# Decay attention with a squared-ReLU MLP on one core: the scores of the first fourteen heads as two rounded products

## The chip, the cores and the metric

The kernel runs on one core of a Trainium2 chip, as one launch. The core has five engines that run side by side and meet only at semaphores: TensorE (PE in the profile; PEld is its weight load), VectorE (DVE), ScalarE (ACT), GpSimd (POOL) and SyncE (SP), which here only issues DMAs. The metric is device time in microseconds for the whole launch, the median of three runs.

## The reference

For 8 batches of 8 heads (64 heads in all, 576 tokens, head size 64) it computes causal attention with a decay, and puts the joined heads through an MLP (4608 tokens, width 512, hidden width 2048):

```
scores = scale * q @ k^T + (cum_i - cum_j)      # cum = cumsum(log(clip(f, 1e-4, 1)))
scores = where(causal, -1e9, scores); scores -= max(scores, -1)
attn = exp(scores);  attn /= sum(attn) + 1e-9;  x = attn @ v
out = relu(x @ w_in) ** 2 @ w_out
```

Everything is float32 for the reader; the two MLP weights arrive as float64 and are turned into float32 inside the kernel.

## The kernel before

**Two kinds of product.** A matmul on float32 tiles goes through PE in several passes, as two MATMUL rows in the profile. A matmul on tiles marked F32R (rounded float32) is a single row, and its operands must have been written in that rounded type. Where a rounded product alone is too coarse, the kernel splits an operand into a rounded part and a rounded remainder and adds several rounded products in the same bank of PSUM. The MLP works like that (line 477: three products for x @ w_in, line 500: three for the second one), and so do all heads from head 14 on.

**Stages.** The work is laid out in slots, six for each head, one for each of six score units (`UNITS`: pieces of 320, 320, 192, 64, 448 and 256 columns, 1600 in all). In slot u of head h the program writes the score unit (line 337, `score`), its exp on ACT (line 362), and two slots later the product with v (line 392, `av_part`). During head h's slots the row maxima of head h+1 are made (`max_units`): six rounded matmuls (line 313), each followed on DVE by a masked maximum (line 319), and five of the results are sent by a small DMA each (line 325) from a column in SBUF into row 66 of the query operand of head h+1. The scores of head h+1 contract over that row too, so that they come out with the maximum already subtracted. Rows 64 and 65 carry the decay sums.

**The first heads.** For heads below `NWHOLE` = 14 the scores are one float32 matmul (line 346) on tiles called `rl`, which SP loads straight from memory (`load_whole`, line 259), plus a small mask matmul (line 348) where the unit crosses the diagonal. The maxima of these heads use a second copy of the same data, `rk`, which a GpSimd DMA rounds on its way (`load_rounded`, line 252). From head 14 on one load (`load`, line 237) brings the raw operands to `qkraw`; `prep` rounds them on DVE (lines 279 and 280) and ACT (281, 284) and makes the remainders on GpSimd (287, 290); the scores are two rounded products (lines 352 and 355).

**Weights.** There are 32 weight blocks of 512 KB. `weight_ops` issues the load of a block on SP (line 172) and converts it in five steps, on ACT (181, 209), DVE (192, 197, 202, 204) and GpSimd (210). `RATES` sets how many steps go into a slot: 1.2 in the slots of heads 0 to 7, 2.5 afterwards until all are done. MLP steps are mixed in from slot 60, the first slot of head 10, when the first batch has been divided by its row sums.

**What sets the order.** PE, ACT, DVE and GpSimd carry out their instructions in the order in which the program writes them (`in_order`). The order of SP is left to the scheduler. A queue works strictly in order: an instruction that waits holds everything behind it.

Of the kernel before, what the change touches and what calls it, by code (L numbers as in the profile page):

```python
# [17 lines left out]
def in_order(tc, engines):  # L18

    last = {}  # L20
    for i in tc.nc.cur_bb.bb.instructions:
# [12 lines left out]
def decay_attention_relu2_kernel(  # L34
# [37 lines left out]

    NWHOLE = 14
# [38 lines left out]
    def f32(x):  # L112
        return x if x.dtype == F32 else x.bitcast(F32)

    def constant_rows(engine, x, ones=True):

        engine.memset(f32(x[D:, 0]), -1.0 / SCALE)
        engine.memset(f32(x[D:, 1]), 0.0)
        if ones:
            k = f32(x[D:, 1])  # L120
            nc.gpsimd.affine_select(
                out=k, in_=k, pattern=[[0, S]], compare_op=ALU.not_equal, fill=1.0, base=-2,
# [11 lines left out]
    def decay():  # L134
        ft, zt, ct = (fr[:NH, i, :] for i in range(3))
        nc.vector.memset(zt, 0.0)
        constant_rows(nc.vector, rounded[0], False)
# [6 lines left out]
        chl = wk.tile([P, 2, S], F32R, name="qkraw", bufs=1)  # L144
        ch, cl = chl[:, 0, :], chl[:, 1, :]
# [8 lines left out]
    for x in vhs:  # L154
        nc.gpsimd.memset(x[:, :, D:D + 2].bitcast(F32), 1.0)
    constant_rows(nc.gpsimd, whole[0])
    constant_rows(nc.gpsimd, rounded[1], False)
    constant_rows(nc.gpsimd, whole[1])
# [5 lines left out]
    def weight_ops():  # L164
# [3 lines left out]
        def stage():  # L168
            i = len(staged)
            if i < NW:  # L170
                raw = staged[i] = wk.tile([P, 2 * DM], I32, name=f"w{i}", bufs=1)
                nc.sync.dma_start(out=raw, in_=(w_in, w_out)[i % 2][i // 2].bitcast(I32))
# [62 lines left out]
    def load(h):  # L235
        raw = wk.tile([P, 2, S], F32, name="qkraw", bufs=1)[:D]
        nc.sync.dma_start(out=raw, in_=qk[h])
        raws[h] = raw

    def load_cum(h, k):  # L240

        if h == 0:
            for i, c in enumerate(cum):
                nc.sync.dma_start(out=f32(k[D + i:D + i + 1, :]), in_=c[h:h + 1])
        else:
            nc.sync.dma_start(out=f32(k[D:D + 2, :]), in_=cum_dr[h])

    def load_rounded(h):

        x = rounded[h % 2]  # L250
        state[h] = dict(r2=x[:, 0], kl0=x[:, 1], p={})
        nc.gpsimd.dma_start(out=x[:D], in_=qk[h])
        if cum:
            load_cum(h, x[:, 1])

    def load_whole(h):

        x = state[h]["whole"] = whole[h % 2]
        nc.sync.dma_start(out=x[:D], in_=qk[h])
        if cum:  # L260
            load_cum(h, x[:, 1])
# [8 lines left out]
    def prep(h, part):  # L270

        if part == 0:
            x = wk.tile([P, 2, S], F32R, name="rl")
            (r2, kl0), (r1, l2) = ((x[:, 0], x[:, 1]) for x in (rounded[h % 2], x))
            st = state[h] = dict(r2=r2, kl0=kl0, r1=r1, l2=l2, p={}, raw=raws.pop(h))
            if h < NWHOLE + 2:
                nc.gpsimd.memset(f32(kl0[D:D + 32]), 1.0)
            load_cum(h, kl0)
            nc.vector.tensor_copy(out=r2[:D], in_=st["raw"][:, 0, :])
            nc.vector.tensor_copy(out=kl0[:D], in_=st["raw"][:, 1, :])  # L280
            nc.scalar.copy(out=st["l2"][D:], in_=st["raw"][:, 1, :])  # L281
        st = state[h]
        if part == 1:
# [430 lines left out]
```

## Time and profile before

| what | value |
|---|---|
| median of 3 runs | 1253.07 us (1252.28 to 1254.52) |
| profiled execution, its own time | 1255.36 us |
| its span, first to last instruction | 1253.3 us |
| busy: PE, DVE, ACT, GpSimd | 95%, 63%, 56%, 30% of the span |
| mean granted TensorE clock | 0.995 |

A row of the timeline reads: start, duration, engine, line, operation, output and input by the program's names, shapes, count (x2 where like rows were joined), and in brackets the idle time of the engine just ahead and what ended it. SPq rows are DMA issues on SP's queue. A row of the stretches reads: from:to, length, then for each engine its busy time and instruction count, the granted clock, the busy share of the DMA engines, and GB/s. A group row reads: line, engine, operation, tiles, shapes, count | busy us, mean ns of one | idle before it.

### The profile page before, as it was taken

To read this page: it belongs to the slowest core of one execution; us is meant where nothing else is said; L and a number is where in the kernel's file an instruction comes from. 1 tells how busy PE (TensorE), PEld (TensorE's weight loads), DVE (VectorE), ACT (ScalarE), POOL (GpSimd) and SP (SyncE) were. 2 spreads that over 40 slices of the span, in tenths; PEclk is the share of its full clock that TensorE was granted. 3 is DMA by queue.
4 is the path that set the end of the run, shared out by engine and by line. 5 is a ranking of instruction groups with operands and counts; after the bars stand their busy time and mean duration, and the time that the engine had idled before them with its cause. 6 is when DMAs were issued, how large, how long until landed. Compare 5 with 4: busy or idle time off the path is not lost.

```text
span 1253.3 us, 23182 instructions
## 1 busy us (share of the span) xinstructions
PE 1193.5 (95%) x7652; PEld 1051.8 (84%) x7652; DVE 785.1 (63%) x2042; ACT 702.0 (56%) x1720; POOL 372.4 (30%) x512
## 2 busy tenths in 40 slices
PE   3877899999999999999999999999999999999998
PEld 2544687888989899999899989998998989999997
DVE  7658776666666767666656566667665766532332
ACT  3545455556666666665565556666666666632332
POOL 4323223333333333333322233334333333200000
PEclk9999999999999999999999999999999999999999
DMA  8857631112121112121201121211121212000000
GB/s 199 193 129 176 177 87 26 51 32 57 41 55 33 48 37 57 40 57 26 55 18 52 31 57 32 55 34 52 40 57 41 57 41 52 17 27 1 18 18 17
DMA packets 115639, 71.90 MB, mean 57 GB/s; under 512 B 97384, under 2 KB 97384, under 8 KB 115520
## 3 DMA queue, kind: packets, MB, share of 16 engines
q1 hardware_dynamic: 114400, 66.30, 21.7%
q0 software_dynamic: 1120, 4.13, 1.5%
q8 instruction: 61, 1.00, 0.3%
q14 instruction: 58, 0.48, 0.1%
HBM read 60.20 MB, written 9.88 MB: 56 GB/s over the span
## 4 chain that ended last, share of the span: by engine, by line
PE 63%; ACT 1%; issue 1%; POOL 1%; DMA 0%; DVE 0%; SPq 0%; POOLq 0%; DVEq 0%; ACTq 0%
PE bank L477 25%; PE bank L500 24%; PE bank L388 3%; PE bank L355 2%; PE bank L390 2%; PE bank L389 2%; PE bank L313 2%; PE bank L352 2%; DMA den<-rdr 0%; ACT ph L377 0%; ACT den L426 0%; ACT r L485 0%; ACT p L362 0%; POOL v L299 0%; ACT rl L281 0%
## 5 line engine op out<-in xcount | busy, mean ns | idle before, releaser
L500 PE MATMUL bank<-w,gh 128*128 128x512 f32 x1152 | 413.8, 400 | 0.0
L477 PE MATMUL bank<-xh,w 128*128 128x256 f32 x2304 | 330.7, 286 | 4.9 <-DVE tcol L319 4.9
L378 DVE TENSOR_TENSOR pl<-p,ph 128x320 fp32r<-128x320 f32 (+4 forms) x300 | 186.9, 623 | 206.6 <-ACT ph L377 197.1
L477 PEld LDWEIGHTS bank<-xh,w 128*128 128x128 f32 x2304 | 301.2, 190 | 13.8 <-DVE tcol L319 5.3
L500 PEld LDWEIGHTS bank<-w,gh 128*128 128x128 f32 x1152 | 217.6, 189 | 39.0
L485 ACT ACTIVATE r<-bank 128x256 f32<-128x256 f32 x288 | 110.4, 383 | 211.7 <-PE bank L477 198.3
L500 PE MATMUL bank<-w,gl 128*128 128x512 f32 x576 | 227.1, 394 | 0.2 <-DVE gl L488 0.2
L486 DVE TENSOR_TENSOR g<-r 128x256 f32<-128x256 f32 x288 | 127.3, 442 | 144.2 <-ACT r L485 143.4
L364 POOL TENSOR_SCALAR_AFFINE_SELECT p<-p 128x128 f32<-128x128 f32 (+1 forms) x250 | 81.5, 326 | 454.2 <-ACT p L362 313.5
L377 ACT CAST ph<-p 128x320 fp32r<-128x320 f32 (+4 forms) x300 | 124.4, 415 | 148.9 <-POOL p L364 147.1
L477 PE MATMUL bank<-xl,w 128*128 128x256 f32 x1152 | 185.3, 283 | 0.0
L319 DVE CUSTOM_DVE_ANT_0 bank<-bank,mz 128x256 f32<-128x256 f32 (+4 forms) x320 | 133.7, 432 | 45.9 <-PE bank L313 44.5
L477 PEld LDWEIGHTS bank<-xl,w 128*128 128x128 f32 x1152 | 158.9, 191 | 0.0
L362 ACT ACTIVATE p<-bank 128x320 f32<-128x320 f32 (+4 forms) x300 | 115.8, 386 | 71.7 <-PE bank L355 67.3
L488 DVE TENSOR_TENSOR gl<-g,gh 128x256 fp32r<-128x256 f32 x288 | 128.9, 448 | 35.7 <-ACT p L362 0.9
L313 PE MATMUL bank<-rk 66*128 66x320 f32 (+9 forms) x384 | 111.8, 318 | 24.8 <-DMA rk<-qkraw 13.4
L487 ACT ACTIVATE gh<-r 128x256 fp32r<-128x256 f32 x288 | 120.5, 418 | 9.1
L500 PEld LDWEIGHTS bank<-w,gl 128*128 128x128 f32 x576 | 109.3, 190 | 14.3 <-DVE gl L488 0.9
L313 PEld LDWEIGHTS bank<-rk 66*128 66x128 f32 (+3 forms) x384 | 68.7, 185 | 40.1 <-DVE tcol L319 17.1
L388 PE MATMUL bank<-pl,vh 128*65 128x320 f32 (+4 forms) x350 | 99.4, 284 | 1.6 <-ACT den L426 1.4
L389 PE MATMUL bank<-ph,v 128*64 128x320 f32 (+4 forms) x350 | 94.8, 271 | 0.0
L390 PE MATMUL bank<-ph,vh 128*65 128x320 f32 (+4 forms) x350 | 93.0, 271 | 0.0
(71 smaller groups left out, 1498.2 us busy)
## 6 DMA issues: line engine op xcount, KB each, us to landing
qkraw<-in_qk SPq DMA_DIRECT2D x50, 288.0 KB
v<-in_v SPq DMA_DIRECT2D x64, 160.0 KB
den<-rdr SPq DMA_DIRECT2D x64, 144.0 KB
out<-osb SPq DMA_DIRECT2D x36, 256.0 KB
w<-in_w_in SPq DMA_DIRECT2D x16, 512.0 KB
w<-in_w_out SPq DMA_DIRECT2D x16, 512.0 KB
rl<-in_qk SPq DMA_DIRECT2D x14, 288.0 KB
rk<-in_qk POOLq DMA_DIRECT2D x14, 288.0 KB, 4.7
```

Source lines behind the costliest of these rows:

```text
L313: nc.tensor.matmul(ps[:m, :n], st["r2"][:rows, q0:q0 + m], st["kl0"][:rows, k0:k0 + n], start=True, stop=True,)
L319: nc.vector.tensor_tensor_reduce(out=ps[:m, :n], in0=ps[:m, :n], in1=mz[:m, mo:mo + n], op0=ALU.add, op1=ALU.min, scale=-1.0, scalar=init, ...
L377: nc.scalar.copy(out=ph[:kn, :n], in_=p[:kn, :n])
L378: nc.vector.tensor_tensor(out=pl[:kn, :n], in0=p[:kn, :n], in1=ph[:kn, :n].bitcast(F32), op=ALU.subtract,)
L388: nc.tensor.matmul(acc[:D + 1, o], vh, pl[:kn, i], start=first, stop=False)
L389: nc.tensor.matmul(acc[:D, o], vl, ph[:kn, i], start=False, stop=False)
L390: nc.tensor.matmul(acc[:D + 1, o], vh, ph[:kn, i], start=False, stop=last)
L477: nc.tensor.matmul(ph[:, :T], w[:, s, cc], x[:, cc, :], start=(cc == 0 and k == 0), stop=(cc == NCC - 1 and k == 2),)
L486: nc.vector.tensor_tensor(out=g, in0=r, in1=r, op=ALU.mult)
L487: nc.scalar.activation(out=gh, in_=r, func=AF.Square)
L488: nc.vector.tensor_tensor(out=gl, in0=g, in1=gh.bitcast(F32), op=ALU.subtract)
L500: nc.tensor.matmul(po, g[:, ts], w[:, s], start=(fc == 0 and k == 0), stop=(fc == NF - 1 and k == 2),)
```

## The change

- The scores of heads 0 to 13 become two rounded products, `kl0` with `r2` over all 128 rows and `l2` with `r1`, with the mask matmul between them where there was one. The product with v of these heads stays float32.
- For heads 0 to 7 (`NDEEP` = 8) the rounded copies `r2` and `kl0` come from GpSimd DMAs, now two for each head, into three sets of tiles instead of two; the raw operands come by `load` into `qkraw` (even heads) or the tile of `xt1` (odd heads). ACT makes two copies and DVE two remainders for each of these heads.
- Heads 8 to 13 are prepared like the later ones: rounded by DVE from the raw load, remainders on GpSimd, and their maxima are made in slots 1.5 to 4 instead of 0 to 2.5.
- `load_whole` and the `rl` tiles of the first heads are gone, and with them 14 loads of 288 KB.
- The 32 weight loads are issued from ACT's queue.
- At the start the constant rows are written in another order, and the DMAs of the decay sums on SP are kept in the order of writing.

```diff
-    rounded = [cpool.tile([P, 2, S], F32R, name=f"rk_{i}") for i in range(2)]
-    whole = [wk.tile([P, 2, S], F32, name="rl") for _ in range(2)]
+    r2s = [cpool.tile([P, S], F32R, name=f"r2_{i}") for i in range(2)] + [spare("xh0")]
+    kl0s = [cpool.tile([P, S], F32R, name=f"kl0_{i}") for i in range(2)] + [spare("xl0")]
...
-                nc.sync.dma_start(out=raw, in_=(w_in, w_out)[i % 2][i // 2].bitcast(I32))
+                nc.scalar.dma_start(out=raw, in_=(w_in, w_out)[i % 2][i // 2].bitcast(I32))
...
+            if h < NDEEP and h % 2:
+                raw = wk.tile([P, NCC, S], F32, name="xt1", bufs=1)[:D, :2]
+            else:
+                raw = wk.tile([P, 2, S], F32, name="qkraw", bufs=1)[:D]
+            nc.sync.dma_start(out=raw, in_=qk[h])
...
+        r2, kl0 = r2s[h % 3], kl0s[h % 3]
+        nc.gpsimd.dma_start(out=kl0[:D], in_=qk[h, :, 1, :])
+        nc.gpsimd.dma_start(out=r2[:D], in_=qk[h, :, 0, :])
...
+        eng = nc.vector if h < NDEEP else nc.gpsimd
         if part == 2:
-            nc.gpsimd.tensor_tensor(out=l2, in0=k, in1=st["kl0"][:D].bitcast(F32), op=ALU.subtract)
+            eng.tensor_tensor(out=l2, in0=k, in1=st["kl0"][:D].bitcast(F32), op=ALU.subtract)
         if part == 3:
-            nc.gpsimd.tensor_tensor(out=r1[D:], in0=q, in1=r1[:D].bitcast(F32), op=ALU.subtract)
+            eng.tensor_tensor(out=r1[D:], in0=q, in1=r1[:D].bitcast(F32), op=ALU.subtract)
...
-        if h < NWHOLE:
-            masked = q0 == k0
-            r, k = st["whole"][:, 0], st["whole"][:, 1]
-            nc.tensor.matmul(ps[:kn, :n], k[:, k0:k0 + kn], r[:, q0:q1], start=True, stop=not masked)
+        rows = P if h < NWHOLE else D + 3
+        nc.tensor.matmul(
+            ps[:kn, :n], st["kl0"][:rows, k0:k0 + kn], st["r2"][:rows, q0:q1], start=True, stop=False,
+        )
+        if h < NWHOLE and q0 == k0:
+            nc.tensor.matmul(
+                ps[:kn, :kn], mz[:kn, MW - P:MW - P + kn], eye[:kn, :kn], start=False, stop=False,
+            )
+        nc.tensor.matmul(
+            ps[:kn, :n], st["l2"][:, k0:k0 + kn], st["r1"][:, q0:q1], start=False, stop=True,
+        )
...
-    SPLIT = 0, 1, 1, 3
-    LOAD = 4
+    SPLIT = (0, 1, 2, 3), (0, 1, 1, 3)
+    LOAD = 3, 4
...
+        deep = h < NDEEP
+        for part in range(4):
+            at((h - 1) * NU + SPLIT[not deep][part], 1, prep, h, part)
+        if h > 1:
+            at((h - 2) * NU + LOAD[not deep], 0, load, h)
+        if deep and h > 1:
+            at((h - 2) * NU, 1, load_rounded, h)
+            at((h - 2) * NU, 1, load_cum, h)
-        for i, x in enumerate(MAXIMA[split]):
+        for i, x in enumerate(MAXIMA[not deep]):
```

How the instructions stand now is shown at three places. The first is SP's queue where it sends the maxima of a head (`tcol` is the column of maxima). Before, during head 2, the maxima of head 3 go into `rl`:

```order
L325 DMA rl<-tcol 1x128x1
L436 DMA cmp<-den 64x1x9 x2
L325 DMA rl<-tcol 1x128x1 x3
L172 DMA w_428<-in_w_in 128x1024
L266 DMA v<-in_v 128x5x64
L325 DMA rl<-tcol 1x64x1
```

Now, during head 2, the same maxima go into `r_0_76` (the query operand of head 3):

```order
L320 DMA r_0_76<-tcol 1x128x1
L256 DMA v<-in_v 128x5x64
L320 DMA r_0_76<-tcol 1x128x1 x2
L427 DMA cmp<-den 64x1x9
L320 DMA r_0_76<-tcol 1x128x1
L320 DMA r_0_76<-tcol 1x64x1
```

The load of v and the weight load no longer stand between the last maxima and their DMA.

The second place is DVE during head 1, from the first maximum of head 2 to the last. Before:

```order
L319 ISA bank_294,tcol<-bank_294,mz 128x256
L319 ISA bank_297,tcol<-bank_297,mz,tcol 128x320
L319 ISA bank_314,tcol<-bank_314,mz 128x448
L319 ISA bank_318,tcol<-bank_318,mz 128x320
L192 TENSOR_SCALAR wmag<-wmag 128x512
L319 ISA bank_330,tcol<-bank_330,mz 128x192
L197 TENSOR_SCALAR osb<-wmag 128x512
L319 ISA bank_341,tcol<-bank_341,mz 64x64
```

Now, with `l_320` and `r_347` the remainder tiles of head 2:

```order
L315 ISA bank_317,tcol<-bank_317,mz 128x256
L315 ISA bank_322,tcol<-bank_322,mz,tcol 128x320
L315 ISA bank_343,tcol<-bank_343,mz 128x448
L315 ISA bank_349,tcol<-bank_349,mz 128x320
L186 TENSOR_SCALAR wmag<-wmag 128x512
L315 ISA bank_362,tcol<-bank_362,mz 128x192
L191 TENSOR_SCALAR osb<-wmag 128x512
L284 TENSOR_TENSOR l_320<-qkraw,xl_81 64x576
L315 ISA bank_374,tcol<-bank_374,mz 64x64
L196 SCALAR_TENSOR_TENSOR osb<-w_177,osb 128x512
L287 TENSOR_TENSOR r_347<-qkraw,r_347 64x576
```

One remainder has come in ahead of the last maximum, the other behind it.

The third place is ACT around the first slots of head 1, where the exps of its first two units (`ph`, `pl`) are made. Before:

```order
L362 ACTIVATE ph<-bank_284 128x320
L425 COPY xt_289<-bank_237 64x320
L426 COPY den<-bank_237 1x320
L209 CAST w_301<-osb 128x512
L362 ACTIVATE pl<-bank_304 128x320
```

Now:

```order
L166 DMA w_304<-in_w_in 128x1024
L353 ACTIVATE ph<-bank_306 128x320
L416 COPY xt_312<-bank_256 64x320
L417 COPY den<-bank_256 1x320
L276 CAST l_320<-qkraw 64x576
L203 CAST w_329<-osb 128x512
L353 ACTIVATE pl<-bank_332 128x320
```

The copy into `l_320` and the weight load `w_304` are new among ACT's exps; the weight casts stood there already. With the waits shown, the weight loads on ACT read like this:

```order
L166 DMA w_248<-in_w_out 128x1024 [waits DMAHW3_49]
L166 DMA w_304<-in_w_in 128x1024 [waits DMAHW1_49]
L166 DMA w_397<-in_w_out 128x1024 [waits DMAHW2_49]
```

Each waits for the end of an earlier DMA on one of eight completion semaphores that ACT's and SP's loads share.

More of the change, by code (lines that the diff above doesn't have):

```diff
@@ L270, in prep @@
     def prep(h, part):
+        if h >= NH:
+            return
         if part == 0:
[L273 to L281, printed above, removed]
+            b = h % 3 if h < NDEEP else h % 2
+            raw = raws.pop(h)
+            if h >= NDEEP:
+                r2, kl0 = r2s[b], kl0s[b]
+                state[h] = dict(r2=r2, kl0=kl0, p={})
+                load_cum(h)
+                nc.vector.tensor_copy(out=r2[:D], in_=raw[:, 0, :])
+                nc.vector.tensor_copy(out=kl0[:D], in_=raw[:, 1, :])
+            st = state[h]
+            st["raw"] = raw
+            st["l2"] = wk.tile([P, S], F32R, name="l2")
+            nc.scalar.copy(out=st["l2"][D:], in_=raw[:, 1, :])
         st = state[h]
+        eng = nc.vector if h < NDEEP else nc.gpsimd
         if part == 1:
+            st["r1"] = wk.tile([P, S], F32R, name="r1")
             nc.scalar.copy(out=st["r1"][:D], in_=st["raw"][:, 0, :])
@@ L323, in unit @@
             if last:
-                r = st["whole"][:, 0] if h < NWHOLE else st["r2"].bitcast(F32)
-                nc.sync.dma_start(out=r[D + 2:D + 3, q0:end], in_=acc)
+                nc.sync.dma_start(out=st["r2"][D + 2:D + 3, q0:end].bitcast(F32), in_=acc)
         us = []
@@ L635, in decay_attention_relu2_kernel @@
     load_f()
+    load(0)
     load_rounded(0)
+    constant_rows(nc.vector, 0)
+    load_rounded(1)
     convert(1)
[L638 removed]
     decay()
[L640 to L641 removed]
+    begin = len(tc.nc.cur_bb.bb.instructions)
+    load_cum(0)
     store_cum()
[L643 to L644 removed]
+    in_order(tc, [mybir.EngineType.SP], begin)
+    load(1)
+    constant_rows(nc.gpsimd, 1, 2)
+    load_cum(1)
+    for x in vhs:
+        nc.gpsimd.memset(x[:, :, D:D + 2].bitcast(F32), 1.0)
     for n in range(-2 * NU, last_slot + 1):
```

82 lines of the change are left out of this document (22 added, 60 removed).

## The prediction

> **What bounds the kernel now.** I read the page first, then cut the span into stretches at the first scores of a head, then followed single heads on the timeline.
>
> ```profile
> PE 1193.5 (95%) x7652; PEld 1051.8 (84%) x7652; DVE 785.1 (63%) x2042; ACT 702.0 (56%) x1720; POOL 372.4 (30%) x512
> PE   3877899999999999999999999999999999999998
> ...
> 0.00:23.00 23.00, 3.04 (x7) 1.58 (x7) 17.54 (x34) 8.25 (x12) 10.84 (x25) 1.00 0.82 212
> 23.00:104.33 81.33, 63.90 (x291) 44.34 (x291) 49.51 (x148) 41.78 (x99) 24.30 (x31) 0.98 0.74 166
> 104.33:127.81 23.48, 18.39 (x75) 11.62 (x75) 20.34 (x46) 13.47 (x30) 8.77 (x10) 0.93 0.66 164
> 127.81:216.06 88.25, 80.49 (x463) 66.43 (x462) 64.87 (x143) 42.33 (x101) 26.93 (x25) 0.98 0.37 97
> 216.06:1253.30 1037.24, 1027.65 (x6824) 927.78 (x6822) 632.89 (x1671) 596.22 (x1480) 301.54 (x423) 1.00 0.16 40
> ```
>
> The 95% for PE is a mean over unlike stages. The five stretches are: the start; heads 0 to 7 (81.33 / 8 = 10.17 us a head); heads 8 and 9, where weight conversion runs at double rate; heads 10 to 13, with MLP steps mixed in; and everything from head 14 on, where PE is busy for 1027.65 of 1037.24 us. In the last stretch nothing but PE work counts. In heads 0 to 7 PE is busy for 79%, so something else ends a wait there. The change touches only the first 216 us.
>
> What a head waits for shows where head 1 ends, and in head 3:
>
> ```profile
> 37.34 0.22 DVE L319 CUSTOM_DVE_ANT_0 bank<-bank,mz 64x64 f32<-64x64 f32 x1
> 37.69 0.60 SPq L266 DMA_DIRECT2D v<-in_v  x1
> 38.38 0.59 SPq L325 DMA_DIRECT2D rl<-tcol  x1
> 39.74 0.51 PE L346 MATMUL bank<-rl 128*128 128x320 f32 x1
> ...
> 45.35 0.22 DVE L319 CUSTOM_DVE_ANT_0 bank<-bank,mz 64x64 f32<-64x64 f32 x1
> 47.62 0.60 SPq L172 DMA_DIRECT2D w<-in_w_in  x1
> 48.32 0.68 SPq L266 DMA_DIRECT2D v<-in_v  x1
> 49.09 0.59 SPq L325 DMA_DIRECT2D rl<-tcol  x1
> 50.13 0.78 PE L346 MATMUL bank<-rl 128*128 128x320 f32 x2 [2.19 <-DMA rl<-tcol]
> 51.55 0.70 PE L346 MATMUL bank<-rl 128*128 128x320 f32 x2
> 51.60 0.43 DVE L319 CUSTOM_DVE_ANT_0 bank<-bank,mz 128x256 f32<-128x256 f32 x1 [2.85 <-PE bank L313]
> 52.09 0.22 PE L348 MATMUL bank<-p,mz 128*128 128x128 bf16 x1
> 55.93 0.21 DVE L319 CUSTOM_DVE_ANT_0 bank<-bank,mz 64x64 f32<-64x64 f32 x1
> 57.00 0.60 SPq L266 DMA_DIRECT2D v<-in_v  x1
> 57.69 0.83 SPq L325 DMA_DIRECT2D rl<-tcol  x1
> 60.17 0.54 PE L346 MATMUL bank<-rl 128*128 128x320 f32 x1 [2.37 <-DMA rl<-tcol]
> ```
>
> It is a loop. Head 3 begins with its first score at 50.13; 1.47 us later DVE starts the first maximum of head 4 (51.60), because that matmul stands behind the score on PE; the last maximum ends on DVE at about 56.2, 4.6 us later; its row goes out on SP only at 57.69, behind the load of v; and when it has landed head 4 begins, 60.17. 1.47 + 4.6 + 4.0 is the 10.04 us of the head. In head 2 the tail from last maximum to next head was 4.5 us (45.6 to 50.13), with a weight load and a v load ahead on SP; at the end of head 1, 37.6 to 39.74, it was 2.1 us.
>
> **The change, part by part.**
>
> *PE.* The rows below give the price of a score unit before and in its new form, as head 14 has it already.
>
> ```profile
> 45.85 0.92 PE L346 MATMUL bank<-rl 128*128 128x448 f32 x2
> 46.60 0.22 PE L348 MATMUL bank<-p,mz 128*128 128x128 bf16 x1
> ...
> 216.06 0.32 PE L352 MATMUL bank<-rk 67*128 67x320 f32 x1
> 216.21 0.31 PE L355 MATMUL bank<-rl 128*128 128x320 f32 x1
> 216.36 0.70 PE L411 MATMUL bank<-ph,v 128*128 128x320 f32 x2
> ...
> 229.95 0.37 PE L352 MATMUL bank<-rk 67*128 67x448 f32 x1
> 230.15 0.37 PE L355 MATMUL bank<-rl 128*128 128x448 f32 x1
> 230.36 0.25 PE L388 MATMUL bank<-pl,vh 128*65 128x192 f32 x1
> ```
>
> Durations of PE rows overlap, so I take start to next start. A float32 unit of 320 columns holds PE from 51.55 to 52.09, 0.54 us, one of 448 from 45.85 to 46.60, 0.75 us: 1.68 ns a column. The pair of rounded products takes 0.30 and 0.41 us, 0.93 ns a column. Over the 1600 columns of a head that is 0.75 ns x 1600 = 1.2 us less. Where PE binds, it is worth 1.2 us a head; elsewhere only the first unit (0.54 - 0.30 = 0.24 us), which stands ahead of the first maximum in the loop.
>
> *Added work.* The rows of the same operations in the later heads and at the start:
>
> ```profile
> L287 POOL TENSOR_TENSOR rl<-qkraw,rk 64x576 fp32r<-64x576 f32 x50 | 72.3, 1445 | 0.2
> L281 ACT CAST rl<-qkraw 64x576 fp32r<-64x576 f32 x50 | 33.5, 670 | 0.7
> L280 DVE CAST rk<-qkraw 64x576 fp32r<-64x576 f32 x50 | 33.5, 669 | 0.0
> L279 DVE CAST rk<-qkraw 64x576 fp32r<-64x576 f32 x50 | 26.0, 520 | 0.0
> L252 POOL DMA_DIRECT2D rk<-in_qk x14 | 8.3, 590 | 14.2 <-PE bank L313 14.2
> 9.14 0.75 DVE L147 TENSOR_TENSOR qkraw<-xt,qkraw 64x576 fp32r<-64x576 f32 x1
> ...
> 145.50 1.26 POOL L210 TENSOR_TENSOR w<-osb,w 128x512 fp32r<-128x512 f32 x1 [9.04 <-ACT w L209]
> 145.66 1.43 DVE L197 TENSOR_SCALAR osb<-wmag 128x512 int32<-128x512 int32 x1
> ```
>
> ACT gets two copies a head (2 x 0.67 = 1.34 us). It also gets the weight loads: 1.2 steps a slot, six slots, five steps a block, so 1.44 blocks a head. The trace has no DMA issue on ACT; bounds are 0 and the 0.6 us of the longer issues on SP and POOL above, so up to 0.86 us a head, and I take 0.6 us each. ACT then has 41.78 / 8 + 1.34 + 0.86 = 7.4 us of work a head. DVE gets two subtractions of 0.75 us for heads 0 to 7: 49.51 / 8 + 1.5 = 7.7 us a head. Both still fit into a head of 9 to 10 us, but with little room. For heads 8 to 13 DVE gets two casts (0.52 + 0.67 = 1.19 us) and GpSimd two subtractions (2.9 us) each; the cost of the latter is also that DVE and GpSimd hold each other up, as in the last two rows, where an operation that elsewhere takes 0.43 us needed 1.43. GpSimd's DMAs for heads 0 to 7 are issued over five slots ahead of use, which covers their 0.59 us each and their landing.
>
> *Start.* PE begins with scores at 23.00. The change takes a weight load and a v load out from between the last rows of head 0 on SP, but puts a subtraction ahead of the last maximum, and makes one row of decay sums wait for the second weight load. I take 0; bounds -2 (three issues of 0.6) and +2 (the tail of 4.5 us instead of 2.1 us).
>
> *Heads 0 to 7.* The first part of the loop becomes 1.47 - 0.24 = 1.23 us; the second 4.6 + 0.75 = 5.35 us, because the first remainder stands ahead of the last maximum. The tail: on SP one `cmp` DMA and the row ahead (0.6 each, partly overlapped by DVE) remain, 0.9 us; from issue to the next head the three heads above took 1.4, 1.0 and 2.5 us; I take 2.0, since the DMA engines stay 74% busy. Tail 2.9 us, head 9.5 us. Against 10.17 that is 8 x -0.68 = **-5.4 us**. Bounds: with the tail of head 1 (2.1) a head is 8.7 us, -11.8; with that of head 3 (4.0) 10.6 us, +3.4.
>
> *Heads 8 and 9.* DVE is busy for 20.34 of 23.48 us and is the bound. Two heads of casts add 2.4 us; four GpSimd subtractions may each hold up a DVE operation by 1 us as above, say half of them, 2 us; some 2.4 of the 3.1 idle microseconds absorb part. **+2 us**, bounds -1 and +5.
>
> *Heads 10 to 13.* PE is busy for 80.49 of 88.25 us, so 4 x 1.2 = 4.8 us less PE work should nearly all arrive; DVE, at 64.87 us, gets 3 x 1.19 more and has room. **-4 us**, bounds -5 and +1 (a stall of DVE or GpSimd that the MLP waits for).
>
> *The rest.* The order of PE from head 14 on is unchanged, so is its length: 0, bounds -1 and +1.
>
> Sum: 0 - 5.4 + 2 - 4 = -7.4 us. Against the profiled execution that is a span of 1253.3 - 7.4 = 1245.9 and a time of 1255.36 - 7.4 = 1248.0. Its own time lies 2.3 us above the median of the runs, so for the median I predict 1253.07 - 7.4 = **1245.7 us**.
>
> One rule stands against the move of the weight loads. The Trainium skill, page "DMA: Bandwidth & Descriptors", section "Issuing engines are not separate DMA queues", says that DMAs started by different engines run on the same sixteen DMA engines and interleave, so that a second issuing engine saves only issue time. By that rule only the 0.6 us of the issue goes from the tail. The trace fits it half: at 0.74 mean busy share a row took 1.0 us to land in one head and 2.5 us in another.
>
> **The rivals.**
>
> *The tail stays (no change).* The row DMAs land as late as in head 3 because the DMA engines are as full as before, from whichever queue. For it: the 2.5 us from 57.69 to 60.17 are landing, not queueing on SP. Against it: 1.0 us in head 2 with a weight load and a v load just ahead. A head takes 10.6 us: +3.4 + 2 - 4 = +1.4, **1254.5 us**. It is also what the skill's rule gives.
>
> *ACT holds the loop (slower).* Place: the weight loads on ACT. They wait for an earlier DMA on a shared completion semaphore, and behind each stand the exps that the product with v and the score banks wait for. Price: with a landing of 1.7 us (mean of 1.0 and 2.5) for each, 1.44 x 1.7 = 2.4 us a head; if half of it delays the loop a head is 9.5 + 1.2 = 10.7 us, +4.2; with +3 and -3 in the next two stretches and +1 at the start, +5.2, **1258.3 us**. It decides from 0.7 us a head on, where 9.5 passes 10.17. For it: ACT has 7.4 us of work in the loop. Against: the DMA waited for was issued most of a head earlier.
>
> *The tail is always short (faster).* All heads like head 1: -11.8, heads 8 and 9 at +1, heads 10 to 13 at -4.8, start -1: -16.6, **1236.5 us**. For it: SP loses six issues in four heads. Against: head 1 was bound by PE, and it had only one DMA ahead on SP.
>
> That the change does not do what it says is excluded by the order: all 32 weight loads stand on ACT, and the float32 score matmuls are gone.
>
> **How the numbers follow.** Forecast 0.45 (its own range 1241 to 1250), no change 0.20, slower 0.20, faster 0.15. I call 0.2%, 2.5 us, what a measurement can tell, so faster is below 1250.6 and slower above 1255.6. Faster: 0.15 + 0.43 = 0.58; the same: 0.02 + 0.16 = 0.18, and 0.02 from the slower case; slower: 0.18 + 0.04 = 0.22. The range reaches to the fast and the slow case: 1237 to 1257 leaves 0.1 on each side.
>
> **What would show it.** Right: first scores of heads 0 to 7 about 9.5 us apart, the subtraction ahead of the last 64x64 maximum, a tail of about 3 us; the stretch from head 10 to head 14 about 4 us shorter; from head 14 on the same 1037 us. Wrong: PE waiting for ACT's exps, ACT idle ahead of a weight load, or heads above 10.2 us apart.

## The result and the profile after

The changed kernel takes 1272.15 us (median; 1269.88 to 1273.47) against 1253.8 us of the kernel before on the same chip. The ratio is 1.0135 (95% interval 1.0104 to 1.0165), so by the ratio it is slower by about 17 us, where 7 us less was forecast and the range ended at 1257. The profiled execution has a span of 1271.1 us, 17.8 more than before.

The busy times, the granted clock and the stretches of the changed kernel, cut at the first scores of heads 0, 8, 10 and 14 as in the prediction:

```profile
PE 1199.7 (94%) x7652; PEld 1060.2 (83%) x7652; DVE 808.9 (64%) x2070; ACT 717.9 (56%) x1748; POOL 388.1 (31%) x523
PEclk9887699999999999999999999999999999999999
...
0.00:25.79 25.79, 3.04 (x7) 1.58 (x7) 13.92 (x32) 8.01 (x12) 11.00 (x24) 1.00 0.83 205
25.79:109.79 84.00, 68.04 (x290) 49.73 (x290) 66.13 (x165) 50.31 (x114) 30.19 (x37) 0.85 0.61 147
109.79:142.94 33.15, 22.13 (x75) 15.31 (x75) 25.46 (x55) 17.41 (x37) 14.55 (x13) 0.65 0.47 133
142.94:237.30 94.36, 81.28 (x460) 67.81 (x461) 74.45 (x149) 46.00 (x106) 33.08 (x28) 0.93 0.26 73
237.30:1271.10 1033.80, 1025.26 (x6824) 925.75 (x6822) 628.96 (x1671) 596.22 (x1480) 299.29 (x423) 1.00 0.16 40
```

Against the stretches before, the start is 2.8 us longer, heads 0 to 7 are 2.7, heads 8 and 9 9.7, heads 10 to 13 6.1 longer, and the rest is 3.4 us shorter. PE is idle for 11.0 of 33.2 us in heads 8 and 9 (before 5.1 of 23.5) and for 13.1 of 94.4 in heads 10 to 13 (before 7.8 of 88.3). The granted clock falls to 0.65 in heads 8 and 9.

**What one profile can tell.** The runs below include kernels that are alike up to head 7, but for a load or a remainder in that head's slots, and so show how far one profile scatters. Heads 0 to 7 took 84.0, 81.0, 79.7 and 80.4 us in four kernels with the change's code there, mean 81.3, and 81.3, 82.6, 83.1, 77.4 and 82.9 in five with the code before, mean 81.5. The start took 24.0 to 25.8 in the first four, mean 24.9, and 22.7 to 25.0 in the others, mean 23.4. The rest took 1033.7 to 1035.9 us in nearly all other kernels; in the profile of before it took 1037.2, with head 17 20.1 us long instead of 18.4. What stands out of this scatter is heads 8 to 13, some 16 us; the start is about 1.5 us longer in the mean, but the two groups overlap. In heads 0 to 7 nothing was won, and nothing that can be told was lost.

**Heads 8 and 9.** Around the preparation of head 9, timeline of POOL, SP, DVE and PE:

```profile
107.14 1.40 POOL L287 TENSOR_TENSOR r<-qkraw,r 64x576 fp32r<-64x576 f32 x1
...
111.67 0.50 SPq L235 DMA_DIRECT2D qkraw<-in_qk  x1
...
116.13 0.45 DVE L271 CAST r<-qkraw 64x576 fp32r<-64x576 f32 x1 [4.29 <-DMA qkraw<-in_qk]
...
117.00 0.38 PE L309 MATMUL bank<-kl,r 66*128 66x256 f32 x1 [1.99 <-DVE kl L272]
```

There is one `qkraw`. It is free for head 9 when GpSimd has read it for head 8 (108.5); the load goes out at 111.67 behind four small DMAs on SP and lands 4.4 us later. VectorE stands still for 4.29 us ahead of its cast, in strict order, with the weight conversion behind it, and PE waits 1.99 us for the second cast, which the first maximum of the next head needs.

**Heads 10 to 13.** Head 11 shows what PE waits for now. Timeline of all engines, the rows of one chain:

```profile
174.82 1.35 POOL L204 TENSOR_TENSOR w<-osb,w 128x512 fp32r<-128x512 f32 x1 [0.64 <-ACT w L203]
174.94 1.54 DVE L271 CAST r<-qkraw 64x576 fp32r<-64x576 f32 x1
176.41 0.44 DVE L272 CAST kl<-qkraw 64x576 fp32r<-64x576 f32 x1
176.99 1.49 POOL L284 TENSOR_TENSOR l<-qkraw,kl 64x576 fp32r<-64x576 f32 x1 [0.81 <-PE bank L402]
177.29 1.47 DVE L191 TENSOR_SCALAR osb<-wmag 128x512 int32<-128x512 int32 x1
178.80 0.66 ACT L175 ACTIVATE wmag<-w 128x512 f32<-128x512 f32 x1 [3.36 <-DVE osb L191]
180.90 0.36 ACT L417 COPY den<-bank 1x256 f32<-1x256 f32 x1
181.32 0.81 PE L402 MATMUL bank<-ph,v 128*128 128x320 f32 x2 [2.33 <-ACT den L417]
```

Two like casts take 1.54 and 0.44 us. The long one meets GpSimd's subtraction and ends 0.3 us after it (176.48 against 176.17), as does line 191 (178.76 against 178.48). ScalarE, in order, waits 3.36 us for line 191 and then has two MLP activations, an exp and two copies to do before the bank is free in which the product with v is to be summed: PE waits 2.33 us. The Trainium skill describes this meeting (page "SBUF — State Buffer", section "Who interferes with whom"): a cast or a tensor_scalar of VectorE can run in a mode that takes the pair of ports shared with GpSimd, and then whichever of the two engines issues first has the pair for its whole instruction, and the other blocks. The ends 0.3 us apart agree.

From the first score of head 10 to that of head 14, the waits (engine and line, what it waited for, us in all, times, longest) and one group of VectorE's weight conversion; first of the kernel before, where that step has line 197, then of the changed kernel, line 191:

```profile
ACT wmag L181 <- DVE osb L197: 21.0, 10, 4.4
...
L197 DVE TENSOR_SCALAR osb<-wmag 128x512 int32<-128x512 int32 x12 | 9.1, 756 | 1.2
```

```profile
PE bank L402 <- ACT den L417: 8.5, 4, 3.0
ACT wmag L175 <- DVE osb L191: 32.3, 11, 4.4
...
L191 DVE TENSOR_SCALAR osb<-wmag 128x512 int32<-128x512 int32 x12 | 11.3, 944 | 1.2
```

Before, no wait of PE for the `den` copy stands in the list; after, it is 8.5 us over four heads. Each of the twelve takes either 0.43 us or, when it meets GpSimd, 1.3 to 1.5 us; the long ones are four before and six after, and the means of 756 and 944 ns count them.

### The profile page after: what moved, and what is told of

The parts are those of the page before. It is cut to its first block, busy times and chain, and to the rows that moved or that the text cites. A ratio compares the mean times of both kernels' runs of the same rounds, so it can differ in the third digit from the quotient of the medians.

```text
span 1271.1 us, 23207 instructions
## 1 busy us (share of the span) xinstructions
PE 1199.7 (94%) x7652; PEld 1060.2 (83%) x7652; DVE 808.9 (64%) x2070; ACT 717.9 (56%) x1748; POOL 388.1 (31%) x523
## 4 chain that ended last, share of the span: by engine, by line
PE 83%; DVE 6%; DMA 4%; ACT 4%; issue 2%; POOL 1%; SPq 0%; DVEq 0%; POOLq 0%; ACTq 0%
PE bank L468 31%; PE bank L491 30%; PE bank L379 4%; PE bank L309 4%; PE bank L346 3%; PE bank L339 3%; PE bank L381 3%; PE bank L380 3%; PE bank L402 2%; DVE osb L191 1%; DVE bank L315 1%; DMA r<-tcol 1%; DMA xh<-tcol 1%; DVE wmag L186 1%; ACT den L417 1%
## 5 line engine op out<-in xcount | busy, mean ns | idle before, releaser
L309 PE MATMUL bank<-kl,r 66*128 66x256 f32 x372 | 114.6, 335 | 34.9 <-DMA kl<-l 18.3
L339 PE MATMUL bank<-r,kl 67*128 67x320 f32 (+1 forms) x372 | 115.4, 310 | 11.5 <-DMA r<-tcol 8.9
L346 PE MATMUL bank<-r,l 128*128 128x320 f32 (+4 forms) x384 | 122.8, 320 | 1.4 <-DVE r L287 1.4
L309 PEld LDWEIGHTS bank<-kl,r 66*128 66x128 f32 x372 | 69.7, 193 | 50.9 <-issue 21.0
```

What stands on the lines that cost most here:

```text
L309: nc.tensor.matmul(ps[:m, :n], st["r2"][:D + 2, q0:q0 + m], st["kl0"][:D + 2, k0:k0 + n], start=True, stop=True,)
L339: nc.tensor.matmul(ps[:kn, :n], st["kl0"][:rows, k0:k0 + kn], st["r2"][:rows, q0:q1], start=True, stop=False,)
L346: nc.tensor.matmul(ps[:kn, :n], st["l2"][:, k0:k0 + kn], st["r1"][:, q0:q1], start=False, stop=True,)
```

## The experiments

Four theories were to be told apart: the queue of the weight loads; the lower clock; the single raw buffer in heads 8 and 9; and the work that came onto ACT, DVE and GpSimd. All ratios are to the kernel before in the same comparison; the changed kernel stands at 1.0135.

### The queue of the weights

```diff
-                nc.scalar.dma_start(out=raw, in_=(w_in, w_out)[i % 2][i // 2].bitcast(I32))
+                nc.sync.dma_start(out=raw, in_=(w_in, w_out)[i % 2][i // 2].bitcast(I32))
```

This is the changed kernel with the loads back on SP (e3_wsp); e4_bwact is the kernel before with the loads on ACT.

> The changed kernel with the weight loads back on SP's queue. If the move to ACT saves what the prediction said (0.6 us and more a head in the tail behind the last maximum): slower by 3 to 7 us, 1275 to 1279. If the loads on ACT hold its exps up (the prediction's slower rival): faster by 3 to 6 us, about 1267. If the queue does not matter: within 2 us of 1272.

> The kernel before with the weight loads on ACT's queue and nothing else changed. The prediction's reasoning (tail shorter by the issue): heads 0 to 7 shorter by 4 to 8 us, total 1246 to 1250. If the queue does not matter: 1252 to 1255. If the loads on ACT hold its exps up: 1256 or more.

Measured: e3_wsp 1.0155 (1.0133 to 1.0176), e4_bwact 1.0040 (1.0024 to 1.0056). In the kernel before the move costs 5 us, about what the rival "ACT holds the loop" asked for; in the changed kernel, moving the loads back gains nothing, so there the rival falls as the cause of the loss. Why the two kernels differ in this was not followed up. The Trainium skill's rule that the prediction weighed (page "DMA: Bandwidth & Descriptors", section "Issuing engines are not separate DMA queues": another issuing engine saves issue time and no more) agrees with e3_wsp, where the other queue brings no time.

### The price of the products, and the clock

e5_bcheap is the kernel before with the first third of a score unit's columns as a float32 product and the other two thirds replaced by one bf16 product of the mask tile (so two thirds of the scores of heads 0 to 13 are left out): PE has about the work of the two rounded products, nothing else changes.

```diff
+            c = n // 3
+            nc.tensor.matmul(ps[:kn, c:n], mz[:, MW - P:MW - P + kn], mz[:, :n - c], start=True, stop=True)
+            nc.tensor.matmul(ps[:kn, :c], k[:, k0:k0 + kn], r[:, q0:q0 + c], start=True, stop=True)
```

> The kernel before, with a third of the columns of each score of heads 0 to 13 as the float32 product and a bfloat16 product of zeros over the other two thirds, so that PE spends about what two rounded products take and nothing else changes (it leaves out two thirds of those scores and lays the mask over them instead of adding it). The prediction's reasoning (less PE work is a gain or nothing): heads 0 to 9 at 102 to 105 us instead of 104.8, heads 10 to 13 at 84 instead of 88.3, total 1246 to 1250. Theory C (the granted clock): the granted clock of heads 0 to 9 falls from 0.97 to 0.8 or less and the stretch grows to 107 to 112 us; total 1250 to 1257.

Measured: 0.9971 (0.9956 to 0.9986), 3.6 us faster (1.8 to 5.5). This is about what the cheaper products can bring without anything else. It does not come where the forecast put it. The stretch from head 10 to head 14 in this profile:

```profile
125.21:212.85 87.64, 77.78 (x484) 65.98 (x484) 66.72 (x145) 42.94 (x101) 26.88 (x24) 0.96 0.36 94
```

It is 0.6 us shorter than before (88.25), where 84 was expected: PE is busy 2.7 us less, and its idle time grows from 7.8 to 9.9 us.

e1_busy is the changed kernel with two idle bf16 products ahead of each score of heads 0 to 9, to hold the clock up:

```diff
+        if h < 10:
+            for _ in range(2):
+                nc.tensor.matmul(ps[:P, :MW], mz[:, MW - P:], mz, start=True, stop=True)
```

> The changed kernel with two idle bfloat16 matmuls of 448 columns put into an unused PSUM bank ahead of each score of heads 0 to 9 (about 0.37 us of PE work a slot, more than the change took away). Theory C (the granted clock): with the lighter scores PE falls under the activity that keeps its clock up; with the idle matmuls the granted clock of heads 0 to 9 goes from 0.64-0.96 back to 0.95 or more, and the stretch of heads 0 to 9 (117.2 us in the changed kernel) gets shorter by 6 to 12 us, although PE has more to do. Rival D (DVE and the raw loads): the clock may rise, but the stretch stays at 117 us or grows by up to 4 us.

Measured: 1.0117 (1.0093 to 1.0142). The interval overlaps that of the changed kernel. The stretches of heads 0 to 7 and 8 to 9 in its profile:

```profile
23.65:108.29 84.64, 77.46 (x386) 51.08 (x387) 66.67 (x168) 50.52 (x115) 29.96 (x37) 0.96 0.57 146
108.29:140.70 32.41, 23.05 (x98) 14.53 (x97) 29.27 (x56) 17.27 (x37) 15.86 (x14) 0.84 0.47 136
```

The clock went from 0.85 to 0.96 and from 0.65 to 0.84, and the stretches kept their lengths (84.6 and 32.4 against 84.0 and 33.2). With more PE work the clock was higher, so here it follows how busy PE is, and raising it gave no time that can be told in heads 0 to 9. Two limits remain: the idle products take PE time themselves, which can hide a small gain, and in heads 10 to 13, where the clock is 0.93 instead of 0.98, no run raised it.

### Remainders and the raw buffer

Three edits of the changed kernel: e2_pool moves the remainders of heads 0 to 7 to GpSimd, e10_dverem those of heads 8 to 13 to DVE, e6_raw2 gives head 9 the second raw buffer.

```diff
-        eng = nc.vector if h < NDEEP else nc.gpsimd
+        eng = nc.gpsimd                                      # e2_pool
+        eng = nc.vector if h < NWHOLE else nc.gpsimd         # e10_dverem
-            if h < NDEEP and h % 2:
+            if h < NDEEP + 2 and h % 2:                      # e6_raw2
```

> The changed kernel, but the two remainders (64x576 subtractions) of heads 0 to 7 on GpSimd instead of VectorE. Theory 'VectorE is the loop': VectorE loses 2 x 0.75 us a head and the part from first to last maximum gets 0.75 us shorter, heads 0 to 7 go from 84.0 to about 78 us, total about 1266. Rival 'VectorE and GpSimd exclude each other': a 1.45 us subtraction on GpSimd holds a VectorE operation up for as long, nothing is won: heads 0 to 7 84 to 90 us, total 1272 to 1278.

> The changed kernel, but the raw q and k of head 9 go to the second buffer as for the odd heads below 8, so that the loads of heads 9 and 10 need not wait until the remainders of the head before have left the single buffer. Theory 'the raw buffer binds heads 8 and 9': the waits of 4.3 and 1.3 us of the casts for that load go, heads 8 and 9 shrink from 33.2 to about 28 us, total about 1267. Rival 'the clock binds' (0.65 of full speed there): no more than 1 us, total 1271 to 1272.

> The changed kernel, but the remainders of heads 8 to 13 on VectorE instead of GpSimd. Theory 'exclusion': a VectorE operation that meets GpSimd's subtraction takes 1.5 us instead of 0.4, ScalarE waits in order for it (3.4 us), and TensorE's product with v waits 1.6 to 2.3 us a head behind ScalarE; without GpSimd's subtractions the stretch of heads 10 to 13 falls from 94.4 to 88 or 89 us, total about 1266. Rival 'VectorE has too much work': 2 x 0.75 us more a head, the stretch grows to 96 or 97 us, total about 1275.

Measured: e2_pool 1.0133 (1.0100 to 1.0166), e6_raw2 1.0075 (1.0047 to 1.0103), e10_dverem 1.0054 (1.0037 to 1.0070). In heads 0 to 7 it does not matter which of the two engines subtracts: what DVE is spared (3.0 us less busy over the eight heads) is no time. In heads 8 to 13 both remedies help, by 7.5 and 10 us, so the GpSimd subtractions and the late raw load are a large part of the loss. The same with both remedies, and with both and the idle products:

> The changed kernel with both remedies: the remainders of heads 8 to 13 on VectorE, and the raw q and k of head 9 in the second buffer. If the two losses (GpSimd's subtractions beside VectorE; the single raw buffer) are separate, their gains of 10.9 and 8.0 us add up: about 1253, as fast as the kernel before. If both cure the same wait (the raw buffer comes free late because GpSimd's remainder reads it late), little is added to the better one: 1259 to 1261.

> The same with two idle bf16 matmuls ahead of each score of heads 0 to 9 as in the earlier run with busy matmuls. Theory 'the clock is a loss of its own': another 5 us below the kernel with both remedies. Rival 'the clock only follows from TensorE's waits': within 1.5 us of it, or slower.

Measured: g1_both 1.0061 (1.0044 to 1.0078), g2_both_busy 1.0053 (1.0037 to 1.0068). The gains do not add. In heads 8 and 9 DVE's waits for the raw load fall from 5.6 us to 1.2 in e10_dverem and go in e6_raw2, so either remedy takes most of the same wait. And with the clock of heads 0 to 7 at 0.98 instead of 0.88 the time is the same. Heads 10 to 13 of g1_both:

```profile
133.51:224.31 90.80, 82.45 (x460) 69.40 (x461) 72.61 (x154) 46.06 (x106) 24.72 (x21) 0.91 0.26 74
```

No remainder of heads 11 to 13 is left on GpSimd there, and the stretch is still 2.6 us longer than before (88.25), though the score products are the cheaper ones. So exclusion by these subtractions is not all of it. In e10_dverem, too, only part of what was expected came: 91.4 us, not 88 or 89.

### Only the heads where PE binds

The kernel before, with the two rounded products only where PE is 91% busy. The rounded operands come from GpSimd's DMA, remainders on DVE, weights on SP. f4_late11 does it from head 11 on, f5_late10 from head 10. The part of the edit that sets the times:

```diff
+        if NFULL <= h < NWHOLE:
+            at((h - 1) * NU, 0, load_rounded, h)
-                at((h - 1) * NU + SPLIT[part], 1, prep, h, part)
+                at((h - 1) * NU + (SPLIT if h >= NWHOLE else (0, 1, 2, 3))[part], 1, prep, h, part)
```

> The kernel before with the two rounded products in heads 11 to 13 alone, rounded operands by GpSimd's DMA issued at the start of the head before, remainders on VectorE, maxima two slots later, weights on SP. Theory 'the price of TensorE counts where TensorE binds': 3 x 1.2 us less, 1250 to 1251. Rival 'ScalarE and VectorE give it back' (two copies of 0.67 and two subtractions of 0.75 us a head): 1253 to 1257.

> The same from head 10 on: 4 x 1.2 us, 1249 to 1250, if TensorE binds in head 10 too; by the trace of before (20.65 us busy of 26.48 there) it does not, then the same as from head 11 on or up to 2 us slower.

Measured: f4_late11 1.0070 (1.0053 to 1.0087), f5_late10 1.0056 (1.0036 to 1.0076). An earlier try, f1_dma10_dve, issued the load of the rounded operands two heads ahead; there the tiles of heads 10 and 11 are overwritten by the loads of heads 12 and 13 while still in use, so its scores are of other operands, the amount of work is the same:

> The kernel before with the two rounded products in heads 10 to 13 alone, where TensorE is busy for 91% of the time; their rounded operands come from GpSimd's DMA as in the kernel before, the remainders are on VectorE, the weight loads stay on SP. Theory 'TensorE's price counts where TensorE binds, if no casts and no GpSimd subtractions come with it': heads 10 to 13 lose up to 4 x 1.2 us, total 1249 to 1250. Rival 'what comes with it on ScalarE and VectorE eats it' (two copies of 0.67 and two subtractions of 0.75 us a head): 1253 to 1256.

Measured: 1.0070 (1.0047 to 1.0093); the first score of head 10 waits 4.67 us for that load. Two of the places where PE waits in f4_late11:

```profile
167.43 0.55 PE L317 MATMUL bank<-rk 66*128 66x256 f32 x1 [3.91 <-DMA rk<-in_qk]
...
211.28 0.81 PE L419 MATMUL bank<-ph,v 128*128 128x320 f32 x2 [1.54 <-ACT den L434]
```

The load goes out late, at 161.13, behind a GpSimd operation that itself waited 5.43 us for a DMA, and in head 13, whose own extra work is nil (head 14 is prepared as before), PE again waits for the `den` copy. DVE comes late into that head: its last conversion step of the head ahead starts at 203.00, with the first score at 203.03; in the kernel before it starts at 194.04, 1.5 us ahead of the score (195.51). f1_dma10_dve and f4_late11 are slower than either of their theories allowed, and f5_late10 is about as slow as f4_late11. Even in the stage where PE is busy for 91%, the cheaper products saved no time; but part of the loss is the late load, which these edits brought, so they do not show what the work on ACT and DVE costs there by itself.

### Each kind of added work alone

This measures the disputed cost by itself: the kernel before, PE's products untouched, and beside them work of the same kind and place as the change adds, whose results nothing reads. It reads the `rl` tiles and waits for their loads. Shortened, with the conditions as remarks:

```diff
+        x, w = scratch[0], state[h]["whole"]
+        q, k = w[:D, 0, :], w[:D, 1, :]
+        nc.scalar.copy(out=x[D:, part, :], in_=(k, q)[part])                                   # h1: 2 in heads 0-13
+        nc.vector.tensor_tensor(out=x[:D, 0, :], in0=q, in1=k, op=ALU.subtract)                # h2: 2 in heads 0-7
+        nc.vector.tensor_copy(out=x[:D, 0, :], in_=q)                                          # h2: heads 8-13
+        nc.vector.tensor_copy(out=x[:D, 0, :], in_=k)                                          # h2: heads 8-13
+        nc.gpsimd.tensor_tensor(out=x[:D, 1, :], in0=q, in1=k, op=ALU.subtract)                # h3: 2 in heads 8-13
```

> The kernel before, to which ScalarE's added copies alone are given: in each of heads 0 to 13 two copies 64x576 whose results nothing reads (28 x 0.67 = 18.8 us of ScalarE). If ScalarE has room, as the forecast took it: +0 to +2 us, 1253 to 1255. If its order is what TensorE waits for: a third or more of the 18.8 arrives, 1259 or more.

> The kernel before, to which VectorE's added work alone is given: two subtractions 64x576 in each of heads 0 to 7, two casts in each of heads 8 to 13, results not read (16 x 0.75 + 12 x 0.6 = 19 us). If each subtraction ahead of the last maximum lengthens the loop: +6 in heads 0 to 7 and +3 to 4 after, about 1263. If it fills idle time: +0 to +2, 1253 to 1255.

> The kernel before, to which GpSimd's added work alone is given: two subtractions 64x576 in each of heads 8 to 13, results not read (12 x 1.45 = 17.4 us on an engine that is 70% idle). Theory 'exclusion': half of the time that VectorE is held up arrives, 1260 to 1263. If only GpSimd's own work counted: no change, 1253 to 1254.

> The kernel before with the three kinds of added work together and the weight loads on ScalarE's queue; TensorE's products as before. If the added work explains the loss and the cheaper products bring the 3.6 us that the kernel with cut products shows, it is slower than the changed kernel by that: 1274 to 1277. If the single raw buffer adds its own 8 us to the changed kernel: 1265 to 1269.

What was added, in the groups of the three kernels (count | busy us, mean ns | idle before):

```profile
L631 ACT CAST qkraw<-rl 64x576 fp32r<-64x576 f32 x28 | 18.8, 670 | 28.8 <-DMA rl<-in_qk 25.9 <-DMA cum_dr<-qkraw 2.6
```

```profile
L633 DVE TENSOR_TENSOR qkraw<-rl 64x576 fp32r<-64x576 f32 x16 | 13.7, 856 | 0.2
L635 DVE CAST qkraw<-rl 64x576 fp32r<-64x576 f32 x6 | 4.3, 716 | 10.1 <-DMA rl<-in_qk 10.1
L636 DVE CAST qkraw<-rl 64x576 fp32r<-64x576 f32 x6 | 2.7, 452 | 0.2
```

```profile
L638 POOL TENSOR_TENSOR qkraw<-rl 64x576 fp32r<-64x576 f32 x12 | 17.8, 1480 | 5.8 <-DMA rl<-in_qk 4.6 <-DMA rl<-tcol 1.1
```

| added to the kernel before | busy us added | ratio (95% interval) | us, ratio x 1254 |
|---|---|---|---|
| ACT's copies (h1_act) | 18.8 | 1.0050 (1.0031 to 1.0068) | +6.3 |
| DVE's subtractions and casts (h2_dve) | 20.7 | 1.0080 (1.0055 to 1.0105) | +10.0 |
| GpSimd's subtractions (h3_pool) | 17.8 | 1.0049 (1.0032 to 1.0067) | +6.1 |
| weight loads on ACT (e4_bwact) | none shown | 1.0040 (1.0024 to 1.0056) | +5.0 |
| all four (h4_all) | | 1.0187 (1.0158 to 1.0216) | +23.4 |

These engines were 30 to 63% busy in the mean, and each addition costs a third to a half of its busy time. The four singles add up to 27.4, the three without the queue to 22.4; all together cost 23.4. The added work explains more than the loss of 16.9; the 6.5 us between would be what the cheaper products, the loads saved and the other order of the maxima give back in sum.

Heads 8 to 13 in one piece, where the loss lies: the kernel before, e5_bcheap (cheaper products alone), h4_all (added work alone), the changed kernel.

```profile
104.33:216.06 111.73, 98.89 (x535) 78.05 (x536) 85.21 (x189) 55.80 (x130) 35.70 (x34) 0.97 0.43 111
101.07:212.85 111.78, 96.59 (x569) 79.51 (x570) 87.76 (x189) 55.87 (x130) 36.00 (x34) 0.92 0.41 109
111.33:239.54 128.21, 107.93 (x536) 83.86 (x535) 99.45 (x201) 63.30 (x143) 51.08 (x44) 0.88 0.35 96
109.79:237.30 127.51, 103.41 (x535) 83.12 (x535) 99.90 (x204) 63.41 (x143) 47.63 (x40) 0.86 0.32 89
```

The cheaper products alone shorten these heads by nothing; the added work alone lengthens them by 16.5 us, as much as the change does (15.8). PE does not wait at the same places in the two: in h4_all mostly for VectorE's maxima, in the changed kernel mostly for the `den` copy and for VectorE's casts.

Two cautions. The added operations wait for their operand's load (25.9 us idle ahead of ACT's copies, 10.1 ahead of DVE's casts), more than those of the change do, so these prices hold the wait too and are upper ones. And a price is not even over the stages: in the profile of h2_dve heads 8 to 13 are 10.1 us longer, though DVE's extra casts are only 7.0 us of work, and heads 0 to 7, with nearly all of the 13.7 us of subtractions, 2.4 us, which one profile cannot tell.

### Exclusion or VectorE's own work

The weight conversion has one GpSimd subtraction a block. k1_bwdve moves it to DVE in the kernel before, one step later; k2_g1wdve the same in g1_both.

```diff
-            nc.gpsimd.tensor_tensor(out=hl[:, 1], in0=w, in1=hl[:, 0].bitcast(F32), op=ALU.subtract)
+            nc.vector.tensor_tensor(out=hl[:, 1], in0=w, in1=hl[:, 0].bitcast(F32), op=ALU.subtract)
```

> The kernel before with the subtraction 128x512 of the weight conversion (GpSimd, 1.3 us, one a block) on VectorE (0.7 us), one step later. Theory 'exclusion': on GpSimd each holds up one VectorE operation by about 1 us, so on VectorE for 0.7 us it costs no more, and up to 0.3 us a block less: 1248 to 1253. Rival 'VectorE's own work binds': 0.7 us a block more in heads 8 to 13 (19 blocks): 1258 to 1265.

> The same edit in the changed kernel with both remedies (1261.7), where VectorE has the remainders of heads 8 to 13 too. 'Exclusion': 1255 to 1261. 'VectorE's own work binds': 1265 to 1272.

Measured: k1_bwdve 1.0010 (0.9993 to 1.0027), no change; k2_g1wdve 1.0065 (1.0043 to 1.0087), as g1_both. The groups of the conversion over the first 230 us, the kernel before ahead of k1_bwdve:

```profile
L197 DVE TENSOR_SCALAR osb<-wmag 128x512 int32<-128x512 int32 x32 | 22.5, 704 | 2.5
L192 DVE TENSOR_SCALAR wmag<-wmag 128x512 f32<-128x512 f32 x32 | 16.8, 523 | 0.0
...
L210 POOL TENSOR_TENSOR w<-osb,w 128x512 fp32r<-128x512 f32 x32 | 41.9, 1309 | 114.6 <-ACT w L209 97.5 <-issue 7.9 <-DMA rl<-tcol 5.2
```

```profile
L188 DVE TENSOR_TENSOR w<-osb,w 128x512 fp32r<-128x512 f32 x32 | 21.9, 685 | 3.1 <-ACT w L218 2.9
L206 DVE TENSOR_SCALAR osb<-wmag 128x512 int32<-128x512 int32 x32 | 13.4, 418 | 0.0
L200 DVE TENSOR_SCALAR wmag<-wmag 128x512 f32<-128x512 f32 x32 | 13.2, 413 | 0.0
```

DVE gets 21.9 us of work and loses 12.7 us of hold-ups in these two lines alone; the time stays. A subtraction on GpSimd beside a busy VectorE is not free, it is paid for on VectorE. It does not help to move it either. Both medians lie between the ranges of the two theories, so neither is decided by them alone. No version here beats the kernel before; only e5_bcheap, which leaves out scores, is faster.

## Why the prediction was wrong

The forecast was a change of -7.4 us; +17 was measured.

**The step that failed** is in *Added work*: "ACT then has 7.4 us of work a head ... DVE 7.7 us. Both still fit into a head of 9 to 10 us, but with little room". A sum of busy times that is below the length of the head was taken as cost nothing but for one 0.75 us subtraction. The runs show 6.3, 10.0 and 6.1 us for the three engines alone, and 23.4 us for all of the added work with the moved loads: in an order that is fixed, an operation and its wait for an operand delay what is queued behind it unless the engine is idle at that place. The loss came in heads 8 to 13, for which the sum had -2 us (+2 and -4) and the profile shows +15.8.

**Heads 10 to 13, -4, measured +6.** "Should nearly all arrive", because PE is busy for 80.49 of 88.25 us. That step failed even without the added work: in e5_bcheap PE's busy time there falls by 2.7 us, not 4.8, and the stretch by 0.6. In the changed kernel PE's busy time does not fall at all (81.28 us, at a granted clock of 0.93 instead of 0.98; the share of the clock was not measured), and ACT's wait for line 191 grew from 21.0 to 32.3 us. In head 12 of the kernel before ACT waited for the same operation 2.6 us, and the product with v lost 0.4 us:

```profile
181.19 0.67 ACT L181 ACTIVATE wmag<-w 128x512 f32<-128x512 f32 x1 [2.58 <-DVE osb L197]
...
182.57 0.36 ACT L426 COPY den<-bank 1x256 f32<-1x256 f32 x1
...
183.03 0.78 PE L411 MATMUL bank<-ph,v 128*128 128x320 f32 x2 [0.39 <-issue]
```

Counted from the first score of the head (174.89 here, 171.85 in head 11 of the changed kernel), PE is ready for this product after 7.8 us before and 7.1 us after, and ACT's copy is done after 8.0 us and 9.4 us: PE comes a little earlier, ACT much later.

**Heads 8 and 9, +2 with a bound of +5, measured +9.7.** The bound counted the casts and hold-ups of 1 us. It left out the wait that the change adds: a raw load into one buffer that GpSimd's remainder must leave first, with DVE in order behind the cast (4.29 us). The rise went down by 3.6 and 3.9 us in the profiles of e6_raw2 and e10_dverem. The rest is the added work: in the profile of h4_all, which adds no load of raw operands, the two heads are 6.9 us longer, above the bound by itself.

**Heads 0 to 7, -5.4, measured 0.** The loop is the right picture, with two terms off. Head 2 after:

```profile
46.26 0.38 PE L339 MATMUL bank<-xh,xl 128*128 128x320 f32 x1 [2.80 <-DMA xh<-tcol]
...
48.18 0.43 DVE L315 CUSTOM_DVE_ANT_0 bank<-bank,mz 128x256 f32<-128x256 f32 x1 [2.66 <-PE bank L309]
...
53.02 0.74 DVE L284 TENSOR_TENSOR l<-xt,kl 64x576 fp32r<-64x576 f32 x1
53.69 0.22 DVE L315 CUSTOM_DVE_ANT_0 bank<-bank,mz 64x64 f32<-64x64 f32 x1
53.99 1.75 DVE L287 TENSOR_TENSOR r<-xt,r 64x576 fp32r<-64x576 f32 x1
...
57.68 0.61 PE L339 MATMUL bank<-r,kl 128*128 128x320 f32 x1 [2.67 <-DMA r<-tcol]
```

The subtraction stands ahead of the last maximum, as forecast. From first score to first maximum it is 1.92 us (forecast 1.23, before 1.47), to the end of the last maximum 5.7 (5.35), the tail 3.8 (2.9). In the mean of heads 1 to 6 the parts are 1.7, 4.3 and 4.3 us in the profile of before and 2.0, 5.6 and 2.5 in that of after: the tail did become shorter, by more than forecast, and the first two parts took it back. How much of their growth is the lower clock was not separated from the idle products' own time; raising the clock gave no time.

**The start, 0 with a bound of +2.** About 1.5 us longer in the mean of several profiles, within the bound. **The rest, 0.** Right: half of the 3.4 us is a slow head in the profile of before, and the rest lies within the scatter.

**The rivals.** "The tail stays" (1254.5) came nearer than the forecast and missed by 17.7 us, "always short" by 35.7. "ACT holds the loop" (1258.3) had the sign and one of the engines, and missed by 13.9; it named the weight loads, which cost 5.0 us in the kernel before, but whose return to SP gains nothing in the changed kernel. Of what would show the forecast wrong, heads further than 10.2 us apart came true in that profile (10.5; 10.2 by the mean of the four), as did PE waiting behind ACT, though for the copy that frees a bank rather than for the exps.

**Still open.** The 6.5 us that h4_all loses beyond the changed kernel exceed the 3.6 of e5_bcheap by 2.9, which the intervals can hide. Heads 10 to 13 of g1_both remain 2.6 us longer than before; ACT's copies and DVE's work could be the reason, but no run took these away there alone. In the profile of k2_g1wdve, where the weights' subtraction has left GpSimd too, the stretch is 88.2 us, as before, so part of it may be that subtraction; the median of that kernel does not show it. Whether the lower clock of heads 10 to 13 costs anything is open.

## What to carry to other kernels

A cheaper product is time only if PE waits for nothing that the preparation of its operands delays: cost the preparation by adding it alone to the old kernel, with unread results, before writing the new one, and make the products cheaper alone to see what they can bring. A busy share of 30 to 87% in a stage says nothing of free time on an engine with a fixed order; here a third to a half of each added microsecond came through, waits for operands included. Where GpSimd and VectorE work side by side, count GpSimd's operations as VectorE's.

## What was not expected of the hardware

A VectorE cast or scalar operation of 0.42 to 0.45 us takes 1.3 to 1.5 when it meets a GpSimd subtraction of 1.3 to 1.5 us, and ends about 0.3 us after it; 12 such subtractions on an engine that was 70% idle cost the kernel 6.1 us. And idle products that raised the granted clock from 0.88 to 0.98 over 80 us left the time as it was (1.0061 and 1.0053).
